# Ones products earlier and in planned waits, copies of transposed q and k in halves, and another written merge order

## The chip, the core and the metric

The kernel runs on one core of one Trainium2 chip. A core has TensorE (PE, matrix products into the PSUM memory), VectorE (DVE), ScalarE (ACT), GpSimd (POOL) and SyncE (SP); the last two issue the DMA transfers here. The metric is the device time in microseconds of one execution, lower is better; runs are compared by their medians.

## The reference, cut to what matters

Attention in which a query sees the 128 keys up to itself and the first four keys, for 4 batches of 8 heads with 768 positions and head size 64; then an MLP mixer on the result, first over positions, then over channels.

```python
def _attn_ref(q, k, v, n_sink, window):          # 4 x 8 x 768 x 64, n_sink 4, window 128
    scores = scale * np.matmul(q, k.transpose(0, 1, 3, 2))
    keep = is_sink | in_window
    scores = np.where(keep, scores, -1000000000.0)
    a = np.exp(scores - np.max(scores, axis=-1, keepdims=True))
    a = a / (np.sum(a, axis=-1, keepdims=True) + 1e-09)
    return np.matmul(a, v)

def _moe_ref(x, w_tok1, w_tok2, w_ch1, w_ch2):   # x: 4 x 768 x 512
    h = np.maximum(x.transpose(0, 2, 1) @ w_tok1, 0.0) @ w_tok2
    u = x + h.transpose(0, 2, 1)
    return u + np.maximum(u @ w_ch1, 0.0) @ w_ch2
```

## The kernel before

Two heads make a pair, so there are 16 pairs, four to a batch. Products take bf16 and sum in float32. For a pair, PE transposes q and k (12 small products each, 64 rows), engines copy the transposed tiles from PSUM into `qT` and `kT`, PE multiplies them into scores for three groups of key blocks (`scores`, `score_sinks`), ACT takes the exponential (L539) into `pT`, and PE multiplies `pT` by `v` with a column of ones appended (`pv`, or `sink_values` and `values`), so that the sum of weights comes along; DVE takes the reciprocal (L647) and scales into `x_sb` (L650). `mix_h` and `mix_u` mix positions, `turned_u` and `transpose_u` turn the result, and `mix_channels` makes the channel products (`v1` with 384 columns, then `out_part` with 512), which are most of PE's work.

PSUM is split into two score tiles `sc` of two banks each and four single banks `mx`. A user of a bank waits until its former readers are done.

The order of instructions is made when the program is built. `Plan` walks through the work with its own costs of each operation (the numbers given to `Op` and `unit`, the extra `SWITCH` when PE passes between 64-row and 128-row work) and emits what it deems ready next. It starts from times at which each engine is taken to be free (`plan.free`, L997). For the first batch, `first_attention` is chosen freely. From then on PE's two streams are joined by a list, `MERGED` (L47): an entry "3/8" puts the side unit 3 (attention and position mixing of the next batch) after 8 units of the main stream (channel mixing of the present one). For DVE, ACT and POOL the plan takes the operation that can begin first; `urgent` decides between equals.

At the start, DVE fills a tile `ones` (L149), and `keep_warm` (L151) makes seven products of it into one `mx` bank, whose result nobody reads. Then come the first pair's q and k transposes (`turn`, L429), additive masks (`masked`, L484) and scores. Raw q and k of the first four pairs arrive over SP's queue, all else over POOL's; w_tok, the weights of `mix_h`, is one of the loads that stand in POOL's queue behind v.

`prepare` (L393) makes the copies of a transposed pair. Up to pair 4 they are halves: `part` 0 and 1 are the two 64-row halves x of the transposed pair, each 384 columns. For later pairs q is copied whole and k is copied whole, 768 columns each, out of one score tile in which x is the bank (`transposed` L447, `turned_bank` L464). After both copies `cleared` (L470) sets a part of the tile to zero.

Of the kernel before, what the change touches and what calls it, by code (L numbers as in the profile page):

```python
# [16 lines left out]
def kernel(  # L17
# [13 lines left out]
    nc = tc.nc  # L31
    B, H, S, D = q.shape
    P = 128
# [7 lines left out]
    NHP = H // 2  # L41
# [3 lines left out]


    MERGED = (  # L47
# [5 lines left out]
    )  # L53
    NQ = 6
    NPT = 3
# [18 lines left out]
    def bank(tag, *shape, dtype=FP32, slot=None):  # L74

        n = given[tag].pop(0) if slot is None else slot
        if tag == "sc":
            return sc[n]
        return psum.tile([P, *shape], dtype, name=f"ps_{tag}", tag=f"{tag}{n}", bufs=1)

    in_order = tc.keep_in_program_order
# [39 lines left out]
    def mm(*args, **kwargs):  # L121
        in_order(nc.tensor.matmul(*args, skip_group_check=True, **kwargs))  # L122
# [4 lines left out]
    def copy(e, out, in_):  # L127
        if e == "ACT":
            in_order(nc.scalar.activation(out, in_, AF.Copy))  # L129
        else:  # L130
            in_order({"DVE": nc.vector, "POOL": nc.gpsimd}[e].tensor_copy(out=out, in_=in_))  # L131
# [10 lines left out]
    done = {}  # L142
    tiles = {}
# [2 lines left out]


    ones = singles.tile([P, 4 * P], BF16)
    in_order(nc.vector.memset(ones, 1.0))  # L149

    def keep_warm(n, slot):  # L151
        ps = bank("mx", 4 * P, slot=slot)
        for _ in range(n):
            mm(ps, ones[:, 0:P], ones, start=True, stop=True)

    keep_warm(7, 0)

# [16 lines left out]
        fill=MASKED, base=0, pattern=[[0, 4], [1, P]], channel_multiplier=-1,  # L174
# [3 lines left out]
        fill=MASKED, base=-1, pattern=[[0, 4], [-1, P]], channel_multiplier=1,  # L178
# [15 lines left out]
    for n in range(4):  # L194
        i, odd = n // 2, n % 2
        rows = slice(D * i + ODD * odd, D * i + ODD * odd + n_sink)
# [25 lines left out]
    PE_OUT = 190.0  # L222
    SWITCH = 95.0
    FIRST = 1800.0
    LANES = 8


# [19 lines left out]
    class Plan:  # L247
# [38 lines left out]
        def other(self):  # L286
            best = None
            queue = False
            for n, op in enumerate(self.pending):
# [5 lines left out]
                r = self.ready(op)  # L295
                if r is not None and len(self.landings) + op.loads > LANES:
                    r = max(r, self.landings[len(self.landings) + op.loads - LANES - 1])
                if r is None:
# [6 lines left out]
                    best = (t, n, e)  # L305
            return best

        def commit_pe(self, op, t):
            for tag, banks in op.need.items():
                given[tag] = [n for _, n in self.slots(tag)[:len(banks)]]  # L310
                for n, readers in zip(given[tag], banks):
                    self.held[tag][n] = readers
            op.fn()
            self.free["PE"] = t + op.cost["PE"] + SWITCH * (op.half != self.half)
            self.half = op.half
            op.done = self.free["PE"] + PE_OUT + SEM
            self.pending.extend(op.then)

        def run(self, first, main, side):
# [5 lines left out]
            while any(first) or main or side or self.pending:  # L325
# [13 lines left out]
                if o is not None and (t is None or o[0] <= t):  # L339
# [4 lines left out]
                    if op.loads:  # L344
                        self.queue = max(self.queue, self.free[o[2]] + FIRST) + op.lag
                        op.done = self.queue + 500.0
# [39 lines left out]
    def piece(ns, fn, deps, need, then, keys=()):  # L386
        op = Op({}, fn, deps, then, size=float(ns))
        op.need, op.keys = need, keys
        return op
# [3 lines left out]
    def prepare(p):  # L393

        kT = kTb[p % NKB]
        parts = 2 if p <= NHP else 1

        def evict(e, n, part):
            name = ("q", "k")[n]
            if n:  # L400
                t = kT
            elif ("qT", p) in tiles:
                t = tiles["qT", p]
            else:
                t = tiles["qT", p] = att_pool.tile([P, S], BF16, name="qT2")
            to = t.rearrange("d (x p j) -> d x p j", x=2, j=NT)
            copy(e, to if parts == 1 else to[:, part], tiles["ps_" + name, p] if parts == 1 else tiles["ps_" + name, p][part])

        free = ([("sk", p - 2)] if p >= 2 else [], [(n, p - NKB) for n in ("s", "sk")] if p >= NKB else [])
        if parts == 2:  # L410
            cost = {"DVE": 540.0, "ACT": 500.0}
        else:
            cost = {"DVE": 950.0} if p < NHP else {"DVE": 950.0, "ACT": 900.0}
        for n, name in enumerate(("qT", "kT")):
            done[name, p] = [
                Op(dict(cost), lambda e, n=n, part=part: evict(e, n, part), free[n]) for part in range(parts)
            ]
            for part, op in enumerate(done[name, p]):
                op.urgent = (3 - part) * (p < NHP)
        tiles["kT", p] = kT  # L420
# [26 lines left out]
    def transposed(p):  # L447

        def run():
            ps = turned_bank(p)  # L450
            for n in range(2):
                for j in range(NT):
                    for x in range(2):
                        rows = ds(D * x, D)
                        in_order(nc.tensor.transpose(ps[:, x, n, j], bfs[p, n][rows, j], ident[rows, rows]))  # L455
                tiles["ps_" + "qk"[n], p] = ps[:, :, n].rearrange("d x j p -> d x p j")

        then = [*done["qT", p], *done["kT", p]]
        then.append(cleared(p, then))
        return piece(  # L460
            350, run, [done["q_bf", p], done["k_bf", p]], {"sc": [then]}, then, [("tq", p), ("tk", p)],
        )

    def turned_bank(key):  # L464

        tiles["ps_turned", key] = bank("sc")
        t = tiles["ps_turned", key].bitcast(BF16).rearrange("d x n b c -> d x n (b c)")[:, :, :, 2 * D:8 * D]
        return t.rearrange("d x n (j p) -> d x n j p", j=NT)

    def cleared(key, readers):  # L470

        op = Op(
            {"DVE": 400.0}, lambda e: in_order(nc.vector.memset(tiles["ps_turned", key][0:D, :, :, 3], 0.0)), readers,
        )
        op.urgent = 2
        return op
# [151 lines left out]
    def sink_values(p):  # L628

        b, hp = pairs[p]  # L630
        vsk = v_sinks[p % NHP]

        def run():
            for i in range(2):
                tiles["ps_o", p, i] = bank("mx", NT, D1)
            for qt in range(2, NT):
                for i in range(2):
                    rows = ds(D * i, D)
                    mm(
                        tiles["ps_o", p, i][:, qt], tiles["pT_sink", p][rows, ts(qt - 2, P)], vsk[rows, i],  # L640
                        start=(qt == 2), stop=False,
                    )

        for i in range(2):
            def recip(e, i=i):
                r = tiles["recip", p, i] = pt_pool.tile([P, NT, 1], FP32, name="recip")
                in_order(nc.vector.reciprocal(r, tiles["ps_o", p, i][:, :, D:D1]))  # L647

            def norm(e, i=i):
                in_order(nc.vector.tensor_tensor(  # L650
                    out=x_sb[b][:, :, ds((2 * hp + i) * D, D)], in0=tiles["ps_o", p, i][:, :, 0:D],
                    in1=tiles["recip", p, i].to_broadcast([P, NT, D]), op=ALU.mult,
                ))

            done["r", p, i] = Op({"DVE": 180.0}, recip)
            done["x", p, i] = Op({"DVE": 550.0}, norm, [done["r", p, i]])
            done["r", p, i].urgent = done["x", p, i].urgent = 3
        return piece(
            120, run, [done["p", p, NT], done["vs", p]], {"mx": [[done[n, p, i] for n in "rx"] for i in range(2)]}, [],
        )  # L660
# [185 lines left out]
    def attention_and_tokens():  # L846

        parts, units = [], []
        first, last = NHP, len(pairs) - 1
        prepare(first)  # L850
        units += [turn(first, n) for n in range(2)]
        for p in range(first, last + 1):
            b, hp = pairs[p]
            pieces = []
            if p < last:
                prepare(p + 1)
                pieces.append(transposed(p + 1))
# [136 lines left out]
        return Op({"POOL": 760.0}, lambda e: fn(), lag=1700.0, loads=1)  # L994

    plan = Plan()
    plan.free.update(PE=3000.0, ACT=2200.0, DVE=3900.0, POOL=4100.0)  # L997
    plan.queue = 14300.0
    plan.landings.append(11500.0)

# [53 lines left out]
    parts = attention_and_tokens()  # L1054
# [40 lines left out]
```

## Time and profile before

| | us |
|---|---|
| median of 3 runs (206.88 to 207.99) | 206.93 |
| the profiled execution's own time | 206.41 |
| its span, first to last instruction | 204.6 |
| PE busy, share of the span | 197.6, 97% |
| ACT busy | 113.8, 56% |
| DVE busy | 112.4, 55% |
| POOL busy | 67.3, 33% |

Busy time is the time in which an engine has an instruction under way. Products on PE overlap, so a busy PE may still stand between products; what tells is the time from the start of one product to the start of the next. In the lists, "x<-y" is what an instruction writes and reads, "L122" a line of the kernel (a helper's line covers all its callers), "x12" how many instructions a row merges, and the bracket says how long the engine was idle before and what ended it.

### The profile page before, as it was taken

How to read it: one execution, taken by the hardware profiler on the slowest of the kernel's cores; microseconds unless marked ns; L12 is line 12 of the kernel's file. 1: busy time of each engine (PE TensorE's matmuls, PEld its weight loads, DVE VectorE, ACT ScalarE, POOL GpSimd, SP SyncE). 2: the span in 40 equal slices, each digit the busy share in tenths (PEclk: the TensorE clock that was granted, in tenths of full speed). 3: DMA queues.
4: the chain of work that ended last, by engine and by line, in shares of the span. 5: the costliest groups of instructions: out<-in, count | busy, mean ns of one | idle time of the engine just before them, and what ended most of it. 6: DMA issues, size and time to landing. Idle time of an engine off the chain costs nothing.

```text
span 204.6 us, 5496 instructions
## 1 busy us (share of the span) xinstructions
PE 197.6 (97%) x2377; PEld 119.3 (58%) x2377; DVE 112.4 (55%) x238; ACT 113.8 (56%) x195; POOL 67.3 (33%) x86
## 2 busy tenths in 40 slices
PE   6798999999999999999999999999999999999994
PEld 2345985566665665667656545666655645665453
DVE  4775653657788766866948557572654361001222
ACT  4898668879706535886563145886750114773000
POOL 6299859795699891450000000000000000000000
DMA  6999999999999999193001112100002112000223
GB/s 193 292 257 188 169 177 191 160 172 206 157 180 189 187 184 198 22 128 20 3 0 54 53 64 97 51 5 0 0 3 103 51 54 103 0 3 0 103 103 103
DMA packets 73223, 21.58 MB, mean 105 GB/s; under 512 B 63216, under 2 KB 70256, under 8 KB 73200
## 3 DMA queue, kind: packets, MB, share of 16 engines
q0 software_dynamic: 67232, 11.80, 73.1%
q1 hardware_dynamic: 5968, 9.45, 13.1%
q8 instruction: 18, 0.29, 0.6%
q14 instruction: 5, 0.04, 0.1%
HBM read 26.75 MB, written 6.29 MB: 161 GB/s over the span
## 4 chain that ended last, share of the span: by engine, by line
PE 85%; DMA 6%; DVE 3%; ACT 2%; POOL 1%; issue 1%; SPq 0%; POOLq 0%; ACTq 0%
PE ps_mx L122 77%; PE ps_sc L122 4%; DMA w_tok<-in_moe_w_tok_dram 4%; DMA v_sink_f<-in_v_dram 2%; PE ps_sc L455 2%; POOL v_aug L115 1%; DVE kT L131 1%; PE ps_mx L427 1%; ACT pT L539 1%; ACT qT L129 1%; PE ps_mx L125 1%; SPq L197 0%; ACT uT L129 0%; DVE u_sb L751 0%; DVE x_sb L650 0%
## 5 line engine op out<-in xcount | busy, mean ns | idle before, releaser
L122 PE MATMUL ps_mx<-uT,w_ch 128*128 128x384 bf16 x384 | 67.1, 326 | 0.1
L122 PE MATMUL ps_mx<-w_ch,v1T 128*128 128x512 bf16 (+2 forms) x312 | 66.9, 363 | 0.0
L539 ACT ACTIVATE pT<-ps_sc 128x1024 bf16<-128x1024 f32 (+1 forms) x48 | 44.4, 952 | 13.0 <-PE ps_sc L122 12.9
L122 PEld LDWEIGHTS <-w_ch 128*128 128x128 bf16 x384 | 36.0, 98 | 23.9 <-issue 1.2
L135 ACT ACTIVATE v1T<-ps_mx 128x384 bf16<-128x384 f32 x77 | 37.7, 490 | 19.5 <-PE ps_mx L122 18.9
L122 PEld LDWEIGHTS <-v1T 128*128 128x128 bf16 x312 | 28.3, 98 | 27.6 <-issue 0.5
L924 DVE TENSOR_TENSOR o_sb<-ps_mx,u_sb 128x512 f32<-128x512 f32 x23 | 15.8, 687 | 34.6 <-PE ps_mx L122 34.6
L122 PEld LDWEIGHTS <-w_tok 128*128 128x128 bf16 x192 | 18.3, 98 | 5.9 <-DMA w_tok<-in_moe_w_tok_dram 0.7
L107 POOL DMA_DIRECT2D q_bf<-in_q_dram x24 | 19.6, 822 | 4.4 <-DMA w_ch<-in_moe_w_ch_dram 2.2
L107 POOL DMA_DIRECT2D k_bf<-in_k_dram x24 | 19.6, 820 | 4.1 <-DMA w_ch<-in_moe_w_ch_dram 1.7
L751 DVE TENSOR_TENSOR u_sb<-ps_mx,x_sb 128x512 bf16<-128x512 f32 x20 | 13.2, 687 | 13.0 <-PE ps_mx L122 12.9
L115 POOL DMA_DIRECT2D v_aug<-in_v_dram x16 | 16.4, 1026 | 8.3 <-ACT v_sink L129 7.1
L131 DVE COPY kT<-ps_sc 128x768 bf16<-128x768 bf16 x11 | 10.5, 958 | 13.4 <-ACT qT L129 13.4
L122 PEld LDWEIGHTS <-pT 128*128 128x128 bf16 x352 | 14.1, 98 | 3.3 <-issue 0.6
L129 ACT ACTIVATE qT<-ps_sc 128x768 bf16<-128x768 bf16 x11 | 8.9, 810 | 12.3 <-PE ps_sc L455 12.1
L122 PE MATMUL ps_mx<-v_aug,pT 128*128 128x65 bf16 x352 | 15.6, 194 | 0.0
L547 DVE TENSOR_TENSOR pT<-pT,mask_main 128x1024 bf16<-128x1024 bf16 (+1 forms) x24 | 14.3, 619 | 1.3 <-ACT pT L539 1.3
L122 PE MATMUL ps_sc<-qT,kT 64*64 64x192 bf16 (+3 forms) x288 | 14.4, 248 | 0.0
L135 ACT ACTIVATE h1T<-ps_mx 128x512 bf16<-128x512 f32 (+1 forms) x8 | 4.1, 517 | 17.1 <-PE ps_mx L122 16.9
L122 PE MATMUL ps_mx<-h1T,w_tok 128*128 128x256 bf16 x96 | 13.2, 273 | 0.0
L137 DVE TENSOR_SCALAR v1T<-ps_mx 128x384 bf16<-128x384 f32 x19 | 10.4, 549 | 4.9 <-PE ps_mx L122 4.9
L122 PE MATMUL ps_mx<-x_sb,w_tok 128*128 128x256 bf16 x96 | 12.0, 273 | 0.5 <-DMA w_tok<-in_moe_w_tok_dram 0.4
(68 smaller groups left out, 156.6 us busy)
## 6 DMA issues: line engine op xcount, KB each, us to landing
out_dram<-o_sb SPq DMA_DIRECT2D x23, 256.0 KB, 2.0
v_aug<-in_v_dram POOLq DMA_DIRECT2D x16, 192.0 KB, 7.2
w_ch<-in_moe_w_ch_dram POOLq DMA_DIRECT2D x8, 384.0 KB, 8.8
q_bf<-in_q_dram POOLq DMA_DIRECT2D x24, 96.0 KB, 6.8
k_bf<-in_k_dram POOLq DMA_DIRECT2D x24, 96.0 KB, 5.9
q_f<-in_q_dram SPq DMA_DIRECT2D x4, 384.0 KB, 5.0
k_f<-in_k_dram SPq DMA_DIRECT2D x4, 384.0 KB, 5.7
w_tok<-in_moe_w_tok_dram POOLq DMA_DIRECT2D x2, 384.0 KB, 7.7
```

The lines of the kernel that those rows point to most:

```text
L107: in_order(nc.gpsimd.dma_start(out=out[:, h], in_=rows[:, h]))
L115: in_order(nc.gpsimd.dma_start(out=v_aug.rearrange("p i t d -> p (i t) d")[:, :, 0:D], in_=v[b].rearrange("h s d -> (h s) d")[2 * hp * S:2 ...
L122: in_order(nc.tensor.matmul(*args, skip_group_check=True, **kwargs))
L129: in_order(nc.scalar.activation(out, in_, AF.Copy))
L131: in_order({"DVE": nc.vector, "POOL": nc.gpsimd}[e].tensor_copy(out=out, in_=in_))
L135: in_order(nc.scalar.activation(out, in_, AF.Relu))
L137: in_order(nc.vector.tensor_scalar_max(out=out, in0=in_, scalar1=0.0))
L455: in_order(nc.tensor.transpose(ps[:, x, n, j], bfs[p, n][rows, j], ident[rows, rows]))
L539: in_order(nc.scalar.activation(part(tiles["pT", p][:, :, ds(2 * g, 2)]), of_keys(tiles["ps_s", p, g])[:, :, 0:width(g)], AF.Exp, scale=scale,
L547: in_order(nc.vector.tensor_tensor(out=pt, in0=pt, in1=m, op=ALU.mult))
L751: in_order(nc.vector.tensor_tensor(out=u_part(b, g, s0, n), in0=tiles["ps_u", b, g, s0], in1=x_sb[b][:, s0:s0 + n, c0:c0 + cn], op=ALU.add,))
L924: in_order(nc.vector.tensor_tensor(out=o_sb.rearrange("p (g c) -> p g c", g=2), in1=u_rows(b, st), in0=tiles["ps_out", b, st].rearrange("p ...
```

## The change

Seven edits:

- The memset of `ones` is split: 128 columns first, the other 384 after the first products are recorded.
- `keep_warm` takes a number of columns and may use 64 rows only. Four products of 128 columns come before the seven of 512.
- `Plan.fill` is new: before each unit that PE begins, up to 8500 ns on the plan's clock, it puts products of ones of 128 columns into the gap that the plan sees, 110 ns to each, into a free `mx` bank, with 64 rows if the work before had 64.
- PE is taken to be free at 4450 ns in place of 3000.
- In `prepare` all pairs are copied in halves, so from pair 5 on as well, out of the score tile.
- `sink_values` gives its reciprocal and scaling the urgency 2, which `cleared` has too, in place of 3.
- `MERGED` is another list.

In the built program PE has 18 more products: 4 of ones before the seven, 3 after them, 7 between the first pair's q and k transposes, 2 behind k, 1 before and 1 behind the second pair's q transposes. The other products of the first 20 us keep their order, as do the loads of SP and POOL. ACT has 20 more instructions, DVE 3 more.

```diff
     MERGED = (
-        "1/0 0/2 2/4 3/8 4/15 5/17 6/17 7/19 8/24 9/25 10/25 11/27 12/27 13/29 14/29 15/30 16/32 17/32 18/35 "
...
+        "0/0 1/3 2/5 3/10 4/17 5/17 6/18 7/21 8/24 9/25 10/26 11/27 12/28 14/30 13/30 15/31 16/32 17/33 18/34 "
...
     ones = singles.tile([P, 4 * P], BF16)
-    in_order(nc.vector.memset(ones, 1.0))
-
-    def keep_warm(n, slot):
-        ps = bank("mx", 4 * P, slot=slot)
+    in_order(nc.vector.memset(ones[:, 0:P], 1.0))
+
+    def keep_warm(n, slot, columns=P, half=False):
+
+        ps = bank("mx", columns, slot=slot)
+        rows = slice(0, D if half else P)
         for _ in range(n):
-            mm(ps, ones[:, 0:P], ones, start=True, stop=True)
-
-    keep_warm(7, 0)
+            mm(ps, ones[rows, 0:P], ones[rows, 0:columns], start=True, stop=True)
+
+    keep_warm(4, 0)
+    in_order(nc.vector.memset(ones[:, P:], 1.0))
+    keep_warm(7, 0, 4 * P)
...
+    FILLED = 8500.0
...
+        def fill(self, t):
+
+            n = int((min(t, FILLED) - self.free["PE"] - 50.0) / 110.0)
+            free = self.slots("mx")
+            if n > 0 and free and free[0][0] <= self.free["PE"]:
+                keep_warm(n, free[0][1], P, self.half)
+
         def commit_pe(self, op, t):
+            self.fill(t)
...
-        parts = 2 if p <= NHP else 1
+        parts = 2
...
-                tiles["ps_" + "qk"[n], p] = ps[:, :, n].rearrange("d x j p -> d x p j")
+                tiles["ps_" + "qk"[n], p] = [ps[:, x, n].rearrange("d j p -> d p j") for x in range(2)]
...
-            done["r", p, i].urgent = done["x", p, i].urgent = 3
+            done["r", p, i].urgent = done["x", p, i].urgent = 2
...
-    plan.free.update(PE=3000.0, ACT=2200.0, DVE=3900.0, POOL=4100.0)
+    plan.free.update(PE=4450.0, ACT=2200.0, DVE=3900.0, POOL=4100.0)
```

8 rows, old and new, of the table MERGED are left out of this document.

## The prediction

> **What bounds the kernel now.** I read the page first (slices and chain), then the timeline of the start, the table of waits, the groups by shape, and the timeline of one attention pair. The page:
>
> ```profile
> span 204.6 us, 5496 instructions
> ...
> PE   6798999999999999999999999999999999999994
> ...
> PE 85%; DMA 6%; DVE 3%; ACT 2%; POOL 1%; issue 1%; SPq 0%; POOLq 0%; ACTq 0%
> ```
>
> TensorE (PE) has no slack from the fourth slice to the last, and 85% of the chain lies on it. A change can win only where PE stands still, or lose where it makes PE stand still. From 30 us on, start-to-start times of products are 163 ns (384 columns) and 216 ns (512 columns), and about 95 ns more at each step between 64-row and 128-row work. Beyond that I count three waits, before the products that start at 70.56, 72.73 and 98.75 us: 0.21, 0.20 and 0.23 us, 0.64 us in all. The first 20 us look different:
>
> ```profile
> 1.46 3.17 PE L122 MATMUL ps_mx<-ones 128*128 128x512 bf16 x7 [1.46 <-DVE ones L149]
> 4.91 0.50 PE L439 MATMUL ps_mx<-ident,q_bf 64*128 64x64 bf16 x12 [0.28 <-ACT q_bf L129]
> 5.64 0.35 PE L439 MATMUL ps_mx<-ident,k_bf 64*128 64x64 bf16 x12 [0.23 <-DVE k_bf L131]
> 5.92 1.04 PE L122 MATMUL ps_sc<-mask_add,ident 128*128 128x512 bf16 x4
> 6.89 0.61 PE L122 MATMUL ps_sc<-qT,kT 64*128 64x256 bf16 x8
> ...
> 18.95 0.83 PE L122 MATMUL ps_mx<-x_sb,w_tok 128*128 128x256 bf16 x6 [0.45 <-DMA w_tok<-in_moe_w_tok_dram]
> ```
>
> The seven products of ones run at 427 ns each, half the later pace; the q transposes still take 0.50 us, the k transposes 0.35: the clock opened between 5.2 and 5.6 us, before any heavy product. The page's granted clock shows 1.00 throughout and doesn't tell this. At 18.95 PE waits for a weight load (0.62 us start to start beyond the product). From the first exponential at 7.33 us ACT is the tighter engine, up to PE's wait:
>
> ```profile
> 7.30:10.00 2.70, 1.78 (x36) 0.90 (x32) 2.00 (x5) 2.67 (x5) 1.17 (x2) 1.00 1.62 276
> 10.00:15.00 5.00, 4.98 (x91) 2.44 (x90) 3.99 (x9) 4.78 (x9) 5.00 (x7) 1.00 1.73 266
> 15.00:20.00 5.00, 4.19 (x66) 2.60 (x65) 2.57 (x7) 4.59 (x7) 5.00 (x7) 1.00 1.73 188
> ```
>
> Columns: stretch, length, busy PE, weight loads, DVE, ACT, POOL. ACT is idle 0.66 us of 12.7. Last, one pair's copies (L131, L129) in the steady part:
>
> ```profile
> 42.97 0.81 ACT L129 ACTIVATE qT<-ps_sc 128x768 bf16<-128x768 bf16 x1
> 43.81 0.96 DVE L131 COPY kT<-ps_sc 128x768 bf16<-128x768 bf16 x1 [2.10 <-ACT qT L129]
> 44.89 0.27 DVE L473 MEMSET ps_sc<- 64x256 f32 x1
> 45.74 1.02 DVE L650 TENSOR_TENSOR x_sb<-ps_mx,recip 128x384 bf16<-128x384 f32 x2
> ```
>
> In the table of waits (total, times, longest) that is
>
> ```profile
> DVE kT L131 <- ACT qT L129: 13.4, 11, 2.2
> ```
>
> and in the groups by shape (busy us, mean ns) halves of such copies stand already:
>
> ```profile
> L131 DVE COPY qT<-ps_mx 128x384 bf16<-128x384 bf16 x4 | 2.2, 554 | 1.2 <-PE ps_mx L439 1.1
> L129 ACT ACTIVATE qT<-ps_mx 128x384 bf16<-128x384 bf16 x6 | 2.8, 489 | 0.8 <-PE ps_mx L439 0.6 <-ACT pT L539 0.2
> ```
>
> The k copy starts 0.04 us after the q copy ends, all 11 times: two readers of one score tile go one after the other. The rows of 384 give the price of a half.
>
> **Part 1: ones and fills.** The memset of ones was 0.485 us for 512 columns; one of 12 columns takes 0.07, so 128 cost about 0.17 (0.83 ns a column) and the first product starts at 1.46 − 0.32 = 1.14. Four products of 128 columns at half pace (107 ns) follow, the last ending 0.31 after its start (512 columns: 0.63): 1.77. The built order makes the next seven wait for PE's own semaphore: 1.82; they take 6 × 0.427 + 0.63 = 3.20: 5.02 (before: 4.63). Three fills wait for these (0.05) and take 0.33 (open clock) to 0.53, and the q transposes wait for them again (0.05): **5.45 to 5.65 in place of 4.91**, although q_bf is ready at 4.85. After twelve transposes (0.19) seven fills end in 6 × 0.056 + 0.22 = 0.56 us, and k waits for them: 6.25 to 6.45 in place of 5.64. Two more fills and a step: masks at 6.7 to 6.9 (5.92), scores and first exponential 0.7 to 0.9 later. Two single fills before the second pair's q and the mask behind it stand in waits for ACT: nothing. Queued behind each fill is all of PE. What it buys, q transposes in 0.35, is in these times.
>
> The ACT chain passes the delay on, less what lies idle: at 18.95 PE would come 0.6 to 0.7 later into a wait of 0.62, so little is lost there; but the mask product that PE reached at 20.05 without waiting needs the exponential that ended at 19.73, some 0.6 us later now: about 0.3 to 0.5 late. I take **+0.4** (bounds 0, if the clock opens at once and w_tok lands as late; +0.9, no cover at all). The second memset makes the DVE's start 0.11 longer; mask_add, SP's four v_sink_f loads and POOL's v_aug and w_tok loads behind it move by at most that (19.02 at the latest), inside the same cover. The order of loads on SP and POOL doesn't change.
>
> In a sentence apart: the Trainium skill (TensorE: Matmul & The Clock Gate, Part 1) says that the gate opens after a busy window of about 3.4 us that runs free of the kernel, so that the opening may come a window later; the one trace fits it (3.7 to 4.1 us after the first product). By that rule the sum would be the rival "late clock" below.
>
> **Part 2: halves.** For 11 pairs q (0.81, ACT) and k (0.96, DVE) become four copies: ACT 0.49, DVE 0.55, ACT 0.50, DVE 0.55. In the built order each waits for the other engine's one before it. So the chain from the end of the transposes is 4 × 0.04 + 2.09 = 2.25 us, before 0.04 + 0.81 + 0.04 + 0.96 = 1.85: **0.4 longer, not shorter**; busy time grows 0.19 (ACT) and 0.15 (DVE) a pair. Meanwhile ACT's next exponential stands behind its second half, and DVE's reciprocals, x_sb and bank memset behind its second. The next to wait is PE's product that needs the bank x_sb empties.
>
> The Trainium skill (PSUM — Partial Sum Buffer, "PSUM bank collisions raise a hardware error") forbids two engines on one bank at once, reads included. The halves lie in two banks, so that rule alone would let ACT and DVE work side by side; the trace shows the serial rule only for whole copies that span both banks. By it the chain would be 1.1: the rival "side by side".
>
> **Part 3: the merge.** The work, the 27 bursts of 64-row work after 30 us and so the steps are the same; only the cover differs. Before, behind the transposes of 42.34, PE had 8 products, 22 values, 8 products and 16 scores until the product at 46.94 that needs the bank: 4.6 us, and x_sb's first copy was out after 3.95. In the new order that pair has scores, sinks, 11 values, 4 products, 11 values, 4 products: 0.46 + 0.22 + 0.24 + 0.32 + 0.65 + 0.32 + 0.65 = 2.8 to 2.9. Needed: transposes 0.52, the chain 2.25, x_sb 0.55 less 0.08 overlap, 0.05: 3.3. **PE waits 0.45.** Two later pairs have 4 products, 11, 4, 11, 4: 3.4 to 3.45 against 3.3 plus a reciprocal and memset (0.3): 0.2 each. The mix behind the 68 us pair is short by 0.1 (was 0.21), the h1T wait of 0.20 stays, the third old wait goes. Sum 0.45 + 0.4 + 0.1 + 0.2 = 1.15, plus about 0.05 for each of four crowded DVE queues: 1.35 against 0.64: **+0.7** (bounds −0.44, both x_sb waits gone; +1.3, twice as much per place).
>
> **Sum.** 204.6 + 0.4 + 0.7 = 205.7 us of span; 1.8 lie around it (the execution's own time is 206.41). The median 206.93 is 0.5 above that execution; I add the difference to the median: 206.93 + 1.1, rounded up for the bounds, which reach further upwards: **208.1**.
>
> **Rivals.**
> *Hidden* (207.3): w_tok lands later in most runs than in this one (they are 0.5 us longer), so the start's 0.4 disappears, and x_sb is chosen sooner: only +0.4 of the merge is left. For it: the w_tok wait of 0.62. Against: exponentials behind it are late as well.
> *Side by side* (206.9, not slower): the halves run in two banks, the chain is 1.1 us, x_sb comes 0.7 sooner than before, both its waits (0.44) vanish, the start gives +0.4 back. It decides once the chain is under about 1.8 us. For it: different banks. Against: 13.4 us of serial waits, and the built order.
> *Late clock* (209.0): the window ends after 8 us. Six mask products at 427 in place of 216 cost 1.3, eleven fills 0.05 each 0.55; of 1.8, half meets the cover that is left: +0.9 over the forecast. Against: earlier, denser products.
> *A better merge* (205.8): all 0.64 goes, and half a microsecond at the start. I see no place for the latter.
>
> **How the numbers follow.** Changes under 0.5%, 1.03 us here, can't be told from none. Forecast 0.56 (own range 207.6 to 208.8; slower 0.42, same 0.14); hidden 0.17 (same); side by side 0.10 (same 0.08, faster 0.02); late clock 0.13 (slower); better merge 0.04 (faster). Slower 0.55, same 0.39, faster 0.06. Range 206.9 to 209.2, which leaves out the last case and the outer halves of two others, about 0.15.
>
> **What would show it.** q transposes at 5.4 to 5.7, k at 6.2 to 6.5, first exponential at 8.0 to 8.3 us; no w_tok wait, a wait for ACT at the mask product near 20.4; qT and kT halves alternating ACT, DVE, ACT, DVE 0.04 us apart; a PE wait for x_sb of about half a microsecond near 47 us and two of 0.2 to 0.3 near 86 and 136. Halves that overlap, q transposes before 5.2, or no new wait after 30 us would make it wrong.

## The result, and the profile after

Over 19 runs of each kernel the changed one takes 208.06 us in the median (207.28 to 209.64), the one before 206.93 us (206.11 to 207.99): ratio 1.0051, 95% interval 1.0034 to 1.0067, so it is slower by 0.7 to 1.4 us. The profiled execution took 207.39 us with a span of 205.5 us (before: 206.41 and 204.6).

The page of the changed kernel, span, busy PE in 40 slices, and the shares of the chain that ended last:

```profile
span 205.5 us, 5538 instructions
...
PE   7899999999999999999999999999999999999994
...
PE 85%; DVE 3%; POOL 3%; ACT 3%; DMA 3%; issue 1%; SPq 1%
```

PE is as full as before and has 85% of the chain as before; the page alone doesn't show where 0.9 us went. The timeline of the start:

```profile
1.06 4.35 PE L122 MATMUL ps_mx<-ones 128*128 128x128 bf16 x14 [1.06 <-DVE ones L149]
5.56 0.35 PE L452 MATMUL ps_mx<-ident,q_bf 64*128 64x64 bf16 x12
5.73 0.55 PE L122 MATMUL ps_mx<-ones 64*128 64x128 bf16 x7
6.34 0.35 PE L452 MATMUL ps_mx<-ident,k_bf 64*128 64x64 bf16 x12
8.12 1.02 ACT L552 ACTIVATE pT<-ps_sc 128x1024 bf16<-128x1024 f32 x1 [0.54 <-PE ps_sc L122]
18.90 0.83 PE L122 MATMUL ps_mx<-x_sb,w_tok 128*128 128x256 bf16 x6
20.47 0.50 PE L122 MATMUL ps_sc<-qT,kT 64*128 64x256 bf16 x6
```

The q transposes come 0.65 us later than before, the first exponential 0.79 later; but the first products of `mix_h` start at 18.90 (18.95 before), now without a wait, and the scores behind them at 20.47 in both kernels. The start's delay is used up there, in this profile. The same stretches as before (stretch, length, busy PE, weight loads, DVE, ACT, POOL) show where:

```profile
7.30:10.00 2.70, 2.19 (x42) 1.21 (x40) 1.12 (x3) 2.16 (x4) 1.71 (x3) 1.00 1.71 264
10.00:15.00 5.00, 4.36 (x76) 2.22 (x74) 4.12 (x9) 5.00 (x9) 5.00 (x7) 1.00 1.80 253
15.00:20.00 5.00, 4.91 (x81) 3.06 (x83) 3.33 (x8) 4.79 (x8) 5.00 (x7) 1.00 1.71 187
```

ACT has 0.51 us less up to 10 us, but from 15 to 20 us it is busy for 4.79 us in place of 4.59, and PE for 4.91 in place of 4.19.

The steady part: one pair's copies and what follows, in the timeline.

```profile
44.27 0.49 ACT L129 ACTIVATE qT<-ps_sc 128x384 bf16<-128x384 bf16 x1
44.79 0.56 DVE L131 COPY qT<-ps_sc 128x384 bf16<-128x384 bf16 x1 [1.79 <-ACT qT L129]
45.26 0.18 DVE L660 RECIPROCAL recip<-ps_mx 128x6 f32<-128x6 f32 x1
45.38 0.49 ACT L129 ACTIVATE kT<-ps_sc 128x384 bf16<-128x384 bf16 x1 [0.62 <-DVE qT L131]
45.90 0.56 DVE L131 COPY kT<-ps_sc 128x384 bf16<-128x384 bf16 x1 [0.46 <-ACT kT L129]
46.38 0.55 DVE L663 TENSOR_TENSOR x_sb<-ps_mx,recip 128x384 bf16<-128x384 f32 x1
46.99 1.47 PE L122 MATMUL ps_mx<-uT,w_ch 128*128 128x384 bf16 x8 [0.41 <-DVE x_sb L663]
```

The four halves run one after the other, 0.03 to 0.04 us apart. (So it is in 8 of the 11 pairs; in the other three, from 68.78, 90.66 and 111.24 us on, ACT copies both halves of k, and the chain takes 1.99 us.) Here the chain takes 2.19 us from 44.27 to 46.46 (before 1.80, from 42.97 to 44.77). Behind it x_sb empties its bank at 46.93, and PE, whose product before started at 46.25 and took 0.16, waits for that from 46.41 on. In the table of waits (total, times, longest):

```profile
DVE qT L131 <- ACT qT L129: 14.9, 11, 2.3
ACT kT L129 <- DVE qT L131: 6.9, 11, 0.6
DVE kT L131 <- ACT kT L129: 4.4, 8, 0.6
PEld L122 <- DVE x_sb L663: 3.0, 6, 0.8
```

The first three lines are the alternation. For PE I count start to start, beyond a product's own time: 0.57 us before the product at 46.99, 0.15 at 71.08 (`mix_h`), 0.20 at 73.25 (`h1T`), 0.32 at 85.50 and 0.32 at 136.20; 1.56 in all against 0.64 before. That is 0.92 us, and the spans differ by 0.9. The table of waits can't be used for this sum: it counts a weight load's wait while earlier products still run.

### The profile page after: what moved, and what is told of

The parts are those of the page before. It is cut to its first block, busy times and chain, and to the rows that moved or that the text cites. A ratio compares the mean times of both kernels' runs of the same rounds, so it can differ in the third digit from the quotient of the medians.

```text
span 205.5 us, 5538 instructions
## 1 busy us (share of the span) xinstructions
PE 197.7 (96%) x2373; PEld 120.5 (59%) x2395; DVE 109.2 (53%) x241; ACT 118.5 (58%) x215; POOL 67.1 (33%) x86
## 4 chain that ended last, share of the span: by engine, by line
PE 85%; DVE 3%; POOL 3%; ACT 3%; DMA 3%; issue 1%; SPq 1%
PE ps_mx L122 76%; PE ps_sc L122 5%; DMA k_f<-in_k_dram 3%; PE ps_sc L468 2%; POOL v_aug L115 1%; PE ps_mx L440 1%; DVE qT L131 1%; DVE kT L131 1%; ACT kT L129 1%; ACT qT L129 1%; ACT v1T L135 1%; POOL w_tok L140 1%; DVE x_sb L663 1%; SPq L94 1%; PE ps_mx L452 1%
## 5 line engine op out<-in xcount | busy, mean ns | idle before, releaser
L122 PE MATMUL ps_mx<-w_ch,v1T 128*128 128x512 bf16 (+2 forms) x294 | 66.1, 362 | 1.2 <-issue 0.5
L135 ACT ACTIVATE v1T<-ps_mx 128x384 bf16<-128x384 f32 x85 | 41.3, 493 | 16.2 <-PE ps_mx L122 15.4
L131 DVE COPY qT<-ps_sc 128x384 bf16<-128x384 bf16 x11 | 6.1, 558 | 14.9 <-ACT qT L129 14.9
L663 DVE TENSOR_TENSOR x_sb<-ps_mx,recip 128x384 bf16<-128x384 f32 x22 | 11.7, 548 | 0.2
L122 PEld LDWEIGHTS <-kT 64*64 64x64 bf16 (+2 forms) x320 | 7.7, 101 | 6.5 <-issue 4.4
L129 ACT ACTIVATE qT<-ps_sc 128x384 bf16<-128x384 bf16 x11 | 5.4, 491 | 9.9 <-PE ps_sc L468 9.7
```

The source lines that it names most:

```text
L135: in_order(nc.scalar.activation(out, in_, AF.Relu))
L663: in_order(nc.vector.tensor_tensor(out=x_sb[b][:, :, ds((2 * hp + i) * D, D)], in0=tiles["ps_o", p, i][:, :, 0:D], in1=tiles["recip", p, i ...
```

## The experiments

Twelve runs, in three groups of four; each group ran on one chip beside the kernel before. Ratios are to that one, with 95% intervals. "This start" below is the ones and fills, "the merge" the list `MERGED` with urgency 2; run 4 has the list alone.

**1. The start undone.**

```diff
-    in_order(nc.vector.memset(ones[:, 0:P], 1.0))
+    in_order(nc.vector.memset(ones, 1.0))
-    keep_warm(4, 0)
-    in_order(nc.vector.memset(ones[:, P:], 1.0))
-            self.fill(t)
-    plan.free.update(PE=4450.0, ACT=2200.0, DVE=3900.0, POOL=4100.0)
+    plan.free.update(PE=3000.0, ACT=2200.0, DVE=3900.0, POOL=4100.0)
```

> The changed kernel with its start undone: seven products of ones of 512 columns only, one memset, no products of ones in planned gaps, PE taken to be free at 3000 ns; copies in halves and the new written merge stay. Theory A (from the trace of the changed kernel: the scores start at 20.47 us there as before, so the start's 0.7 us is taken up by the wait for w_tok and the one for POOL's k_bf; the whole loss of 0.9 us lies in PE's waits near 46.5, 85 and 136 us): still slower than before by 0.9 us, ratio to before 1.004 to 1.005, first exponential back near 7.33 us, the same waits at 46.5, 85 and 136 us. Theory B (the prediction's sum: the start carries 0.4 of the 1.1 us): slower than before by 0.7 us, ratio 1.003, that is 0.4 us faster than the changed kernel.

Measured: 207.79 us, ratio 1.0056 (1.0042 to 1.0070), +0.99 us. The steady waits are all there (0.56, 0.15, 0.20, 0.31, 0.31). So halves and merge lose about 1 us without the new start, as theory A has it; B's 1.003 lies outside the interval. What the start adds to that is not settled: the two ratios, 1.0051 and 1.0056, leave it open to about half a microsecond either way. And the first exponential did not come back to 7.33. The timeline of this run:

```profile
5.55 0.50 PE L449 MATMUL ps_mx<-ident,k_bf 64*128 64x64 bf16 x12 [0.24 <-DVE k_bf L131]
5.98 1.89 PE L122 MATMUL ps_sc<-mask_add,ident 128*128 128x512 bf16 x4
7.80 1.03 PE L122 MATMUL ps_sc<-qT,kT 64*128 64x256 bf16 x8
8.45 1.02 ACT L549 ACTIVATE pT<-ps_sc 128x1024 bf16<-128x1024 f32 x1 [1.47 <-PE ps_sc L122]
```

With the very start of the kernel before, the masks take 1.89 us in place of 1.04: products still ran at half pace here up to 8 us and more (scores of 1.03 us in place of 0.61), while in the profile before the k transposes at 5.64 us already took 0.35.

**2. The start alone, old merge, whole copies.** The kernel before with the start's lines of the diff.

> The kernel before with the start's edits alone (four products of 128 columns, split memset, products of ones in the planned gaps, PE free at 4450 ns); whole copies from pair 5 on, the old merge and urgency 3. Theory A: the q transposes start 0.6 us later (5.5 us), the wait before the product at 18.95 us goes, the scores behind it start at 20.4 to 20.5 us as before, time the same within 0.15 us, ratio 1.000. Theory B: 0.4 us slower, ratio 1.002, since the exponentials of the first pairs have no slack (ACT idle 0.66 us of 12.7).

Measured: 207.87 us, ratio 1.0058 (1.0040 to 1.0076), +1.07 us. Both theories missed. The records place the profile's loss exactly, since all instructions from 21 us on are those of the kernel before in the same order: from 21 to 53 us every one of DVE and ACT is 0.55 us later, from 57 us to the end 1.18. The first step is w_tok, which landed at 19.45 us (18.91 before); the second is a landing too (timeline):

```profile
52.96 0.81 PE L122 MATMUL ps_mx<-w_ch,v1T 128*128 128x512 bf16 x3
...
54.25 0.81 PE L122 MATMUL ps_mx<-w_ch,v1T 128*128 128x512 bf16 x3 [0.48 <-DMA w_ch<-in_moe_w_ch_dram]
```

A part of w_ch landed at 54.21 us, 3.40 later than before (50.81), and PE stood 0.64 us for it. This second step came in no other of the profiles below.

**3. Halves alone, and 4. the merge alone.** The kernel before with, first,

```diff
-        parts = 2 if p <= NHP else 1
+        parts = 2
-                tiles["ps_" + "qk"[n], p] = ps[:, :, n].rearrange("d x j p -> d x p j")
+                tiles["ps_" + "qk"[n], p] = [ps[:, x, n].rearrange("d j p -> d p j") for x in range(2)]
```

and, second, only the new list. The expectation for this second run says urgency 2 as well, but the kernel that ran has urgency 3; so no run tells what urgency 2 does by itself.

> The kernel before with the copies in halves alone (all pairs in two halves each of q and k, 384 columns); old start, old merge, urgency 3. Theory A (the four halves serialise, 0.4 us longer than the two whole copies, and the merge was written for one length of that chain, so that the two edits of the merge and the halves only fit each other): new waits of PE behind the old merge, 1 to 1.7 us slower than before, ratio 1.005 to 1.008, most of it before the first product of mix_h near 71 us, whose x_sb comes late on DVE. Theory B (the costs add: halves 0.1 to 0.3 alone, the merge the rest): ratio 1.000 to 1.0015.

> The kernel before with the new merge and urgency 2 alone; whole copies from pair 5 on and the old start. Theory A (merge and halves fit only each other; the wait near 46.5 us belongs to the merge, which puts too few products behind three short pairs, and stands with whole copies too): wait of about 0.5 us near 46.7 us, a long one before mix_h near 71 us, 1.2 to 1.6 us slower than before, ratio 1.006 to 1.008. Theory B (costs add; the wait near 46.5 us comes from the 0.4 us longer chain of the halves): 0.5 to 0.7 us slower, ratio 1.003, the wait near 46.5 us down to 0.1 to 0.2.

Measured: halves alone 208.88 us, 1.0092 (1.0077 to 1.0108); merge alone 208.79 us, 1.0096 (1.0076 to 1.0117). Each alone costs 2.0 to 2.1 us, twice what both cost together. The costs do not add, as theory A has it for both; its sizes were too low (1 to 1.7 us and 1.2 to 1.6 us). Halves alone, timeline near 71 us:

```profile
70.42 0.49 ACT L129 ACTIVATE kT<-ps_sc 128x384 bf16<-128x384 bf16 x1 [0.62 <-DVE qT L131]
...
70.95 0.56 DVE L131 COPY kT<-ps_sc 128x384 bf16<-128x384 bf16 x1 [0.45 <-ACT kT L129]
71.42 0.55 DVE L660 TENSOR_TENSOR x_sb<-ps_mx,recip 128x384 bf16<-128x384 f32 x1
...
72.30 0.53 DVE L660 TENSOR_TENSOR x_sb<-ps_mx,recip 128x384 bf16<-128x384 f32 x1
...
72.89 0.50 PE L122 MATMUL ps_mx<-x_sb,w_tok 128*128 128x256 bf16 x3 [0.62 <-DVE x_sb L660]
```

The last half of k stands on DVE ahead of both x_sb, and `mix_h` waits 0.78 us for the second (0.21 before). That is only a part of the 1.77 us by which this run's steady part is longer, not most of it as theory A had it: PE also stands 0.62 us before the `mix_h` product at 56.32 and some 0.4 us before scores at 38.25, where the kernel before does not wait. In the changed kernel the plan gives both k halves of this pair to ACT, and the same row reads:

```profile
69.89 0.87 ACT L129 ACTIVATE kT<-ps_sc 128x384 bf16<-128x384 bf16 x2 [0.63 <-DVE qT L131]
69.99 1.02 DVE L663 TENSOR_TENSOR x_sb<-ps_mx,recip 128x384 bf16<-128x384 f32 x2
```

The merge alone, near 47 us, with whole copies:

```profile
45.92 0.96 DVE L131 COPY kT<-ps_sc 128x768 bf16<-128x768 bf16 x1 [2.10 <-ACT qT L129]
46.80 0.18 DVE L657 RECIPROCAL recip<-ps_mx 128x6 f32<-128x6 f32 x1
47.03 0.27 DVE L483 MEMSET ps_sc<- 64x256 f32 x1
47.22 0.53 DVE L660 TENSOR_TENSOR x_sb<-ps_mx,recip 128x384 bf16<-128x384 f32 x1
...
47.80 0.66 PE L122 MATMUL ps_mx<-uT,w_ch 128*128 128x384 bf16 x3 [0.41 <-DVE x_sb L660]
```

The wait near 47 us is 0.57 us here as well, so with this list it stands without the halves. That the two figures are equal is chance. From the end of the transposes to the start of x_sb it takes 2.24 us here and 2.22 in the changed kernel, by two ways: the whole copies are done 0.40 us sooner, but behind them DVE still has the reciprocal and the bank's memset ahead of x_sb; in the changed kernel the reciprocal runs between DVE's two halves (45.26) and the memset behind x_sb. The large wait of this run is 0.87 us before `mix_h` at 72.61, where the whole copy of k stands on DVE ahead of both x_sb:

```profile
70.43 0.96 DVE L131 COPY kT<-ps_sc 128x768 bf16<-128x768 bf16 x1 [1.63 <-ACT qT L129]
...
71.53 1.02 DVE L660 TENSOR_TENSOR x_sb<-ps_mx,recip 128x384 bf16<-128x384 f32 x2
...
72.61 0.50 PE L122 MATMUL ps_mx<-x_sb,w_tok 128*128 128x256 bf16 x3 [0.71 <-DVE x_sb L660]
```

In the changed kernel ACT has both halves of k there and DVE is free for x_sb at 69.99; the wait is 0.15 us.

**5. The kernel before once more.**

> The kernel before once more, unchanged, for its spread and a second profile. Theory A (the clock of PE opens at a moment that the kernel with the old start does not set: in the profile on record k's transposes take 0.35 us, the masks 1.04 and the first exponential starts at 7.33 us, in three other profiles with the old start 0.50, 1.89 and 8.45 to 8.93 us): this profile may be of either kind; with the late clock the masks take 1.89 us, the first exponential starts at 8.4 us or later and the span is 0.4 us longer than 204.6. Theory B (the late clock belongs to the edits of those three kernels): 0.35, 1.04 and 7.33 us again. Ratio 1.000 in both.

Measured: ratio 1.0014 (0.9992 to 1.0036). The clock opened early (k 0.35, masks 1.04, first exponential 7.16), but w_tok landed at 19.38 us, and everything from 21 us on is 0.48 us later than in the profile before. So the late clock was not seen in this unchanged kernel. That it is no work of halves or list is argued, not shown: the kernels of experiments 1, 3 and 4 have the same instructions on PE up to the masks as the kernel before. But their three profiles come from one chip and this one from another, so the chip is a rival that no run rules out.

**6. Only the short ones products, no fills.** As 2, without the call of `fill`.

> The kernel before with the split memset and four products of 128 columns ahead of the seven of 512, and no products in planned gaps; all else old. Theory A (the start's edits alone cost 1.1 us because the planned products hold PE up until the q transposes start 0.65 us later, and because the old merge then meets the landing of w_ch): q transposes at 4.85 to 4.95 us, clock open by the k transposes (0.35 us), first exponential at 7.3 to 7.6 us, time 0 to 0.4 us faster than before, ratio 0.998 to 1.000. Theory B (any start but the old one delays the loads of POOL's queue, with the planned products or without): w_tok at 19.4 us or later, a wait for w_ch near 53 us, ratio 1.004 to 1.006.

Measured: 206.78 us, ratio 0.9983 (0.9965 to 1.0001). q transposes at 4.85 us in 0.35, first exponential at 7.26, w_tok at 18.59: theory A.

**7. The fills without the three ahead of q, and 8. five long products in place of seven.** As 2, with

```diff
-    plan.free.update(PE=4450.0, ACT=2200.0, DVE=3900.0, POOL=4100.0)
+    plan.free.update(PE=4850.0, ACT=2200.0, DVE=3900.0, POOL=4100.0)
```

and, for the other, `keep_warm(5, 0, 4 * P)`.

> The kernel before with the start's edits, but PE taken to be free at 4850 ns, so that the three products of ones ahead of the q transposes fall away and the eleven others in planned gaps stay; old merge, whole copies. Theory A: q transposes at 4.9 us, k transposes at 5.7 to 5.9 us (seven products and the emptying of PE's pipe between), first exponential at 7.5 to 7.8 us, ratio 0.999 to 1.002. Theory B (the products in the gaps cost more than they take and the loads are late with any new start): ratio 1.004 to 1.006.

> The kernel before with the start's edits, but five products of 512 columns instead of seven (0.85 us less of ones); old merge, whole copies. Theory A: q transposes at about 4.9 us, clock open by the masks (1.04 us) as the ones still run without a break, first exponential at 7.5 to 7.8 us, ratio 0.999 to 1.002. Theory B (the loads are late with any new start): ratio 1.004 to 1.006, with a wait for w_ch near 53 us.

Measured: 207.83 us, 1.0034 (1.0013 to 1.0056), and 207.80 us, 1.0033 (1.0013 to 1.0052). Both lie between the two theories, and both are slower than run 6 on the same chip, with intervals that don't meet. The first profile has the late clock (masks 1.89, first exponential 9.39) and is 1.28 us late from 21 us on. The second has the early one (exponential 7.33, 0.31 late, w_tok at 19.03); its execution, 206.97 us, was the shortest of its 12, so it doesn't tell what lengthens the others. What the fills did there in most runs stays open.

A part of it may lie at the other end of the kernel. In all five profiles of kernels with fills (runs 2, 7, 8, the changed kernel here and in run 9) the page's list of DMA queues has one packet of instructions more than in the other nine; it starts at 200.5 to 201.5 us, beside the last stores of the output. Changed kernel first, then the kernel before:

```profile
q8 instruction: 19, 0.31, 0.6%
...
q8 instruction: 18, 0.29, 0.6%
```

In these five the last store of 256 KB lands 2.58 to 3.40 us after its issue, in the other nine 2.04 to 2.05. In runs 7, 8 and 9 the span ends 3.44, 3.44 and 3.55 us after the start of PE's last product, in all others 3.16 to 3.18, so up to 0.4 us of these spans is spent there. That the packet is what delays the stores fits all 14 profiles, but no run tested it.

**9. The changed kernel once more, 10. without fills.** For 10, the changed kernel without the call of `fill`.

> The changed kernel once more, unchanged, on the same chip as the three runs beside it and for a second profile. Theory A (what is lost or won in the first 20 us passes one to one to the end, and it is the moment of the clock and the landing of the loads that spread it; the steady part is fixed): from 30 us on the same waits (0.57 near 46.5, 0.15 and 0.20 near 71 and 73, 0.32 each near 85 and 136 us), all times of DVE and ACT from 21 us on shifted by one constant against the first profile, between 0 and 1 us; ratio to before 1.004 to 1.008. Theory B (the waits of the steady part vary too, for instance for w_ch): shifts that grow after 30 us.

> The changed kernel without the products of ones in planned gaps (14 of the 18 new ones); the four of 128 columns ahead of the seven, halves and new merge stay. Theory A (each group in a gap holds PE's next work up by the emptying of its pipe, while the ones alone won in the kernel before): q transposes at 4.85 us, first exponential at 7.3 to 7.6 us, 0.2 to 0.9 us faster than the changed kernel, the four waits of the steady part as there; ratio to before 1.002 to 1.005. Theory B (the start is absorbed by the wait for w_tok): as slow as the changed kernel, 1.005 to 1.006.

Measured: 207.67 us, 1.0035 (1.0016 to 1.0055); without fills 207.62 us, 1.0024 (1.0005 to 1.0044). The second profile of the changed kernel has all its instructions from 21 us on 0.04 to 0.07 us earlier than the first, with the same five waits: the steady part is fixed, theory A (its ratio was a little high). Its span is 0.3 us longer all the same, 205.8 in place of 205.5, all of it behind PE's last product (see run 8). Without fills k comes at 5.48 instead of 5.78 us and the first exponential at 7.17 instead of 7.56, but w_tok landed at 19.16, and the two medians can't be told apart, which is nearer to theory B.

**11. Halves with a repaired merge.** As 10, with 45 entries of the list moved:

```diff
     MERGED = (
-        "0/0 1/3 2/5 3/10 4/17 5/17 6/18 7/21 8/24 9/25 10/26 11/27 12/28 14/30 13/30 15/31 16/32 17/33 18/34 "
...
+        "0/0 1/1 2/4 3/10 4/16 5/18 6/18 7/21 8/24 9/25 10/26 11/27 12/28 15/30 14/30 13/31 16/32 17/33 18/34 "
+        "19/36 20/39 21/39 22/39 23/41 26/42 25/42 24/42 27/44 28/52 29/54 30/54 31/56 32/59 34/61 33/61 36/65 35/66 38/68 "
+        "37/70 39/71 40/72 42/73 43/76 41/76 44/80 46/80 45/80 47/83 48/86 49/86 50/86 51/87 52/94 54/97 53/97 55/97 56/102 "
+        "58/102 57/102 60/105 59/107 62/107 61/112 63/113 67/116 64/121 65/128 68/129 66/132 69/133 70/136 71/139 72/140 73/141 74/143"
```

> As the run before it (halves, ones without planned gaps), but the merge has 45 of its 75 entries shifted by one to a few units or swapped with a neighbour, chosen so that more channel products stand between a pair's products and the next user of its bank. Theory A (the halves by themselves cost nothing; the loss sits in PE's waits behind a merge with too short a cover): the waits near 46.5, 85 and 136 us are gone, 0.9 to 1.0 us faster than the run before it, ratio to before 0.997 to 1.000. Theory B (the halves cost DVE and ACT 0.4 us a pair, whatever the order): waits come back at other places, at most 0.3 us faster than the run before it.

Measured: 206.45 us, ratio 0.9970 (0.9951 to 0.9988), 1.17 us faster than run 10 and 0.57 faster than before. The pair near 44 us again (timeline; lines stand one higher here):

```profile
43.55 0.29 PE L121 MATMUL ps_mx<-v_sink,pT_sink 64*128 64x65 bf16 x8
...
43.76 1.47 PE L121 MATMUL ps_mx<-uT,w_ch 128*128 128x384 bf16 x8
...
45.07 0.84 PE L121 MATMUL ps_mx<-v_aug,pT 128*128 128x65 bf16 x22
...
45.75 2.11 PE L121 MATMUL ps_mx<-uT,w_ch 128*128 128x384 bf16 x12
46.27 0.56 DVE L661 TENSOR_TENSOR x_sb<-ps_mx,recip 128x384 bf16<-128x384 f32 x1
```

Eight products stand ahead of the values and twelve behind, where the changed kernel had four in the middle of the values and four behind, and x_sb is late for nobody. The waits near 46.5, 85 and 136 us are gone; 0.15, 0.20 and one of 0.12 at 138 us are left. The halves are in it as before, with chains of 2.19 us: with this list PE no longer waits behind them near 46.5, 85 and 136 us.

**12. Whole copies with a repaired old merge.** As 6, with 57 entries of the old list moved by one to a few units or swapped (the expectation counts 55).

> The kernel before with the four short ones products and the split memset, whole copies from pair 5 on, and the old merge with 55 of its 75 entries shifted by one to a few units or swapped, chosen to take away the waits at 70.6, 72.7 and 98.8 us. Theory A: those three waits (0.64 us) gone and one of about 0.15 us near 54 us in their place, 0.3 to 0.7 us faster than before, ratio 0.9965 to 0.9985. Theory B (a merge written for one set of times meets others on the chip): new waits elsewhere, ratio 0.999 to 1.003.

Measured: 207.01 us, ratio 1.0006 (0.9983 to 1.0029), between the theories. In its profile the three old waits are gone and one of about 0.3 us stands near 55, but the start is 0.91 us late (w_tok landed at 19.50 us).

All profiles in one table. Behind the kernel's name stand the four masks' time, the first exponential's start, w_tok's landing, and under "turn of u" the start of the first product that turns u (the end of the first batch); "steady" is from there to the start of PE's last product, all in us.

| kernel | masks | exponential | w_tok | turn of u | steady |
|---|---|---|---|---|---|
| before | 1.04 | 7.33 | 18.91 | 26.70 | 174.76 |
| before, again (5) | 1.04 | 7.16 | 19.38 | 27.18 | 174.74 |
| start alone (2) | 1.04 | 8.11 | 19.45 | 27.25 | 175.38 |
| ones alone (6) | 1.04 | 7.26 | 18.59 | 26.63 | 174.76 |
| later fills (7) | 1.89 | 9.39 | 19.38 | 27.98 | 174.74 |
| five ones (8) | 1.04 | 7.33 | 19.03 | 27.01 | 174.75 |
| halves alone (3) | 1.89 | 8.86 | 19.60 | 27.45 | 176.53 |
| merge alone (4) | 1.89 | 8.93 | 19.27 | 27.52 | 176.41 |
| old start, halves, merge (1) | 1.89 | 8.45 | 18.78 | 27.13 | 175.61 |
| changed | 1.04 | 8.12 | 18.69 | 26.70 | 175.65 |
| changed, again (9) | 1.04 | 7.56 | 18.86 | 26.66 | 175.62 |
| changed, no fills (10) | 1.04 | 7.17 | 19.16 | 26.96 | 175.62 |
| repaired merge (11) | 1.04 | 7.26 | 18.88 | 26.68 | 174.37 |
| whole, repaired (12) | 1.04 | 7.47 | 19.50 | 27.61 | 174.47 |

The last column is a property of the program: it repeats within 0.04 us wherever copies and merge are the same, but for the landing of w_ch in run 2. The turn of u moves by 1.35 us over the 14 profiles, by 0.48 between the two of the kernel before, and goes to the start of PE's last product one to one; the 0.3 to 0.4 us at the end in runs 7, 8 and 9 come on top.

## Why the prediction was right, and where it was not

The time was right (208.1 predicted, 208.06 measured, own range 207.6 to 208.8), but its two terms were each off, in opposite directions. That it came within 0.04 us is partly luck: the steady part explains 0.9 of the 1.13 us between the two medians, and where the rest arises in most runs no profile shows.

**Part 1, the start (+0.4 predicted, 0.0 found at the turn of u against the profile before).** The times of its own steps were right in the first profile: q at 5.45 to 5.65 predicted, 5.56 found; k 6.25 to 6.45, found 6.34; masks 6.7 to 6.9, found 6.71; exponential 8.0 to 8.3, found 8.12; no wait for w_tok. The step that failed is the next: that the mask product reached at 20.05 us would wait 0.3 to 0.5 us for the exponential. That row of exponentials, which ended at 19.73 us before, ended at 20.00, 0.27 late and not 0.6, for ACT closed idle time that the kernel before had (0.40 us ahead of 18.00); the mask product stood some 0.07 us for it, and the scores started at 20.47 in both. In the second profile (run 9) the steps themselves came sooner: q at 5.00, k at 5.78, the exponential at 7.56 us. The prediction had named q before 5.2 as a sign against it; the clock opened there during the sixth long product of ones (next start after 0.27 us in place of 0.43), which comes near the condition of its lower bound, and the turn of u was 26.66. The lower bound of 0 was the one to take at either moment of the clock: the table shows that with an early clock the first product of `mix_h` starts 0.04 to 0.05 us after w_tok has landed, or at PE's own arrival when that is later, whether the first exponential came at 7.2 or at 8.1. Across runs the term is not settled: changed against old start with the same halves and merge, 1.0051 and 1.0056 with intervals of about 0.0015 either side, on different chips; against the second profile of the kernel before, the changed one is even 0.5 us early at the turn of u. And the fills may cost at the end of the kernel, which the prediction did not consider (up to 0.4 us, run 9).

**Part 2, the halves (0.4 longer in the chain).** Right: 2.19 us against 1.80, serial, alternating in 8 of 11 pairs, 1.99 in the other three. What the prediction did not see is that their cost depends on the list: alone +1.77 us in the steady part, with the new list less than none (+1.65 for the list without them, +0.86 with them and urgency 2, whose share is not known). With the repaired list and the halves the steady part is 0.39 us shorter than before. The prediction also missed what the halves give: a gap on DVE for the reciprocal, and pairs whose k goes to ACT alone.

**Part 3, the merge (+0.7 predicted, +0.92 found).** Right in mechanism and place: near 47 us 0.45 predicted and 0.57 found, two of 0.2 to 0.3 near 86 and 136 found as 0.32 each, the mix 0.1 and found 0.15, h1T 0.20, the third old wait gone. The size is low by 0.2: the named places came to 1.56 us in place of 1.15, all but h1T a little more than reckoned, and the 0.2 added for four crowded DVE queues has no place of its own. At 47 us, from the transposes at 43.64, PE had 2.77 us of work (2.8 to 2.9 reckoned) and the bank was free after 3.35 (3.3). The reason given there, the halves' chain of 2.25 and x_sb behind it, fits this kernel; it is not the only way to that wait, as run 4 has the same 0.57 with whole copies.

**The rivals.** *Side by side* is excluded by the alternation. The Trainium skill (PSUM — Partial Sum Buffer, "PSUM bank collisions raise a hardware error") forbids two engines on one bank, and the halves lie in two; this program nevertheless lets each engine wait for the other one's half, so that the rule's freedom is not used (waits of 14.9, 6.9 and 4.4 us in the table above). *Hidden* had the outcome right for the start, though not its reason (w_tok landed sooner here, at 18.69 us, not later), and was wrong for the merge. *Late clock* describes what can happen, but not these two profiles: masks of 1.89 us came in three of five profiles with the old start and in one of nine with the short products ahead. Those three are from one chip, so that this count doesn't show that the short products bring the opening forward. The Trainium skill (TensorE: Matmul & The Clock Gate, "Part 1: The HAM clock gate") says that the window is free-running and the count of slow products varies from run to run; the 14 profiles agree that the moment varies, from before 4.07 us (short products 0.06 us apart from there on, run 8) to after 8 us (masks from 6.92 us on in 1.89, run 7); that the window is free-running none of them can show. *A better merge* does not describe the change, but exists: run 11.

## What to carry to other kernels

When two edits belong together, undoing one shows what the pair depends on, not what that edit costs: halves and list cost 2 us each alone and 1 us together (with urgency 2). A written order should be judged by PE's start-to-start gaps, and by who stands ahead of the instruction that empties the bank on its own engine; moving 45 entries of the list was worth 1.2 us with the same work. And a start should be compared over several profiles: here landings and the moment of the clock moved the end of the first batch by 0.48 us between two profiles of one kernel, and by 1.35 us over all fourteen, more than the whole effect under study. Products added at the start should be looked for at the end as well: here they went with one more packet of instructions beside the last stores.

## What the runs showed of the hardware that was not expected

The clock's opening is not in the page: its granted clock reads 1.00 in all profiles, also while products of 512 columns start 427 ns apart in place of 216. It shows only in row times, masks of 1.89 in place of 1.04 us. The landing of w_tok, with the same loads in the same order on the same queues, spread from 18.59 to 19.60 us over 14 profiles (issued at 10.85 to 12.77 us, landed 6.7 to 7.8 us later), and once a part of w_ch landed 3.40 us later than in the kernel before although its own issue was only 1.56 us later (43.70 and 42.14 us). Every trace but the first lacks 20 to 22 of PE's product records (2373 of 2395 in the changed kernel's, whose weight loads are all there); such a gap reads 216 or 226 ns and is no wait.
